# The ninth tile of a pair: two full matmuls into one PSUM bank, and one order for odd and even steps

## Chip, cores, metric

One core of a Trainium2 chip. The metric is the device time of one launch in microseconds (us), the median over runs.

Engine names in the profile: PE is TensorE (PEld its weight loads), DVE VectorE, ACT ScalarE, POOL GpSimd. PSUM is the memory that TensorE writes its products to, in banks; VectorE and ScalarE empty it. A packed matmul uses only part of TensorE's rows or columns (64\*64, 64\*128 or 64\*32 in the profile's rows, against 128\*128 for a full one); going from one of these sizes to another is called a mode switch below.

## The reference, cut to what matters

For 8 batches of 8 heads, 576 positions and head size 64, a memory attention with 32 slots per head, then a layer norm and a feed-forward block over the 512 joined channels, with a residual:

```python
k_m = einsum('bhsm,bhsd->bhmd', a, k)      # a: softmax of phi over positions
v_m = einsum('bhsm,bhsd->bhmd', a, v)
attn = softmax(q @ k_m.T / 8)              # 576 x 32 for each head
x = (attn @ v_m)                           # joined over heads: 8 x 576 x 512
out = x + relu(layernorm(x) * g @ w_ch1) @ w_ch2     # 512 -> 2048 -> 512
```

## The kernel before

It runs in one step per batch. A pair of batches has 2 x 576 = 1152 positions, that is nine tiles of 128. Even steps do tiles 0 to 3, odd steps 4 to 8; hence the "ninth tile" in each odd step. Tile 4 lies across the two batches. A step first makes the hidden layer of its batch (`h_ps`, `mm1`), then for each of its tiles the second product (`ch_ps`, 16 matmuls in two halves, `half(i)`), and in between the attention of the next batch. PSUM is held as two rings: "big" of three buffers of two banks, "one" of two buffers of one bank.

```python
def big(shape, dtype, name):
    return psum.tile(shape, dtype, name=name, tag="big", bufs=3)
def one(shape, dtype, name):
    return psum.tile(shape, dtype, name=name, tag="one", bufs=2)

def x_tiles(pr, ts, stats=True, o_ps=None):        # x of one or two tiles
    n = len(ts)
    if o_ps is None:
        o_ps = big([P, 2, 512], FP32, "o_ps")
    for i, t in enumerate(ts):
        # ... parts: (batch, first and last column, partition offset)
        for g in range(2):
            for (b, a, z, po) in parts:
                s = st8[b]
                for u in range(2):
                    r = 64 * u
                    ov = o_ps[po:po + z - a, u, 256 * i:256 * (i + 1)]
                    nc.tensor.matmul(
                        ov.rearrange("p (j e d) -> p j e d", e=2, d=D)[:, :, g, :],
                        s["Eh"][r:r + 64, g, a:z],
                        s["vb"][r:r + 64, g, 2 * u:2 * (u + 1), :].rearrange("p j d -> p (j d)"),
                        start=True, stop=True, tile_position=(r, po))
    x = moe.tile([P, 2, C], FP32, name="x_sb", bufs=4)
    nc.scalar.activation(out=..., in_=..., func=AF.Copy)      # o_ps to x
    # ...

# ... in the loop over the steps:
half(0)
if more and odd:                     # more: there is a next batch
    o_ps = big([P, 2, 512], FP32, "o_ps")
    kv_ps = big([P, 2, 512], FP32, "kv_ps")
    a_sum(nb, kv_ps)                 # next batch: two small full matmuls
    x_tiles(pr, t[0:2], False, o_ps)
    a_pool(nb, kv_ps)                # 72 packed matmuls; VectorE empties kv_ps
else:
    if more:
        a_kv(nb)                     # a_sum and a_pool
    x_tiles(pr, t[0:2], False)
x_tiles(pr, t[2:4], False)
if odd:
    x_tiles(pr, t[4:5], False)       # the ninth tile
# ... loads
half(1)
x_stats(pr, t[0]); x_stats(pr, t[1]); x_rstd(pr, t[0:2])
if more:
    a_tr(nb)                         # three transposes (kvT_ps)
mm2_out(pr, t[0])                    # VectorE empties the first tile's ch_ps
half(2)
```

`vb` holds zeros outside each head's own block, so contracting over all 128 rows gives the same as contracting each half of 64 rows for its own columns.

The softmax here doesn't subtract the row's maximum and nothing guards it: scores larger than these inputs give would overflow.

## Time and profile before

| | before |
|---|---|
| time | 250.63 us (250.14 to 250.96, 3 runs) |
| TensorE / VectorE / ScalarE busy | 95% / 63% / 52% |
| odd step's stretch, from the batch sums to the second half | 2.21 us |
| even step's | 1.64 us |

The change touches the odd step's stretch, and its like in the last step, which has no next batch. The lines behind the table are in the prediction.

### The profile page before, as it was taken

How to read it: one execution, taken by the hardware profiler on the slowest of the kernel's cores; microseconds unless marked ns; L12 is line 12 of the kernel's file. 1: busy time of each engine (PE TensorE's matmuls, PEld its weight loads, DVE VectorE, ACT ScalarE, POOL GpSimd, SP SyncE). 2: the span in 40 equal slices, each digit the busy share in tenths (PEclk: the TensorE clock that was granted, in tenths of full speed). 3: DMA queues.
4: the chain of work that ended last, by engine and by line, in shares of the span. 5: the costliest groups of instructions: out<-in, count | busy, mean ns of one | idle time of the engine just before them, and what ended most of it. 6: DMA issues, size and time to landing. Idle time of an engine off the chain costs nothing.

```text
span 248.8 us, 5860 instructions
## 1 busy us (share of the span) xinstructions
PE 236.5 (95%) x2460; PEld 132.2 (53%) x2491; DVE 156.0 (63%) x304; ACT 130.0 (52%) x219; POOL 60.7 (24%) x100
## 2 busy tenths in 40 slices
PE   7979899999999999999999999999999999999994
PEld 2544554457544665467544674466544764476442
DVE  3247663685577656687569637685679538783641
ACT  3164572587554465837472656655580755465310
POOL 8643241022325402090206202170205001000000
PEclk9999999999999999999999999999999999999999
DMA  7999999998499799919965997429983301203133
GB/s 150 190 202 206 207 256 213 286 223 148 119 174 236 116 216 245 179 20 194 262 122 117 146 242 168 104 37 221 211 167 68 73 14 43 45 12 75 42 84 84
DMA packets 42451, 36.82 MB, mean 148 GB/s; under 512 B 17461, under 2 KB 37689, under 8 KB 42425
## 3 DMA queue, kind: packets, MB, share of 16 engines
q0 software_dynamic: 17776, 19.53, 46.9%
q1 hardware_dynamic: 24488, 16.79, 28.4%
q8 instruction: 19, 0.31, 0.5%
q10 hardware_dynamic: 160, 0.13, 0.2%
q14 instruction: 8, 0.06, 0.1%
HBM read 41.42 MB, written 9.44 MB: 204 GB/s over the span
## 4 chain that ended last, share of the span: by engine, by line
PE 77%; DMA 17%; issue 2%; ACT 2%; POOL 1%; DVE 0%; POOLq 0%
PE ch_ps L481 45%; PE h_ps L411 22%; DMA q_bf<-in_q_dram 8%; DMA w1r<-in_moe_w_ch_dram 6%; DMA kv_bf<-in_k_dram 3%; PE w1b_ps L390 3%; PE o_ps L442 2%; PE last_ps L493 1%; ACT x_sb L448 1%; PE sc_ps L328 1%; PE den_ps L359 1%; PE kv_ps L210 1%; POOL q_bf L92 1%; PE qT_ps L310 0%; ACT qT L313 0%
## 5 line engine op out<-in xcount | busy, mean ns | idle before, releaser
L481 PE MATMUL ch_ps<-w2b,rT 128*128 128x512 bf16 x531 | 123.0, 379 | 2.3 <-issue 1.6
L481 PEld LDWEIGHTS <-rT 128*128 128x128 bf16 x560 | 52.1, 98 | 63.5 <-issue 6.5
L411 PE MATMUL h_ps<-Eh,w1b 128*128 128x288 bf16 x512 | 66.4, 285 | 1.3 <-ACT rT L417 1.0
L417 ACT ACTIVATE rT<-h_ps 128x576 bf16<-128x576 f32 x88 | 52.2, 648 | 26.8 <-PE h_ps L411 26.8
L411 PEld LDWEIGHTS <-w1b 128*128 128x128 bf16 x512 | 49.5, 97 | 18.1 <-issue 2.4
L394 DVE SCALAR_TENSOR_TENSOR w1b<-m_sb,rsum,w1b_ps 128x512 bf16<-128x512 f32 (+1 forms) x66 | 44.2, 726 | 8.5 <-PE w1b_ps L390 6.1
L419 DVE TENSOR_SCALAR rT<-h_ps 128x576 bf16<-128x576 f32 x40 | 30.3, 758 | 25.2 <-PE h_ps L411 24.6
L505 DVE SCALAR_TENSOR_TENSOR x_sb<-ch_ps,rstd,x_sb 128x512 f32<-128x512 f32 x35 | 26.1, 745 | 9.5 <-PE ch_ps L481 6.4
L461 DVE BATCH_NORM_STATS2 bst<-x_sb 128x6 f32<-128x512 f32 x36 | 24.3, 676 | 6.4 <-ACT x_sb L448 6.4
L448 ACT ACTIVATE x_sb<-o_ps 128x1024 f32<-128x1024 f32 (+1 forms) x20 | 17.8, 939 | 16.1 <-PE o_ps L442 16.0
L287 POOL TENSOR_TENSOR vb<-v,vmask 128x256 bf16<-128x256 bf16 x12 | 7.8, 664 | 60.9 <-DVE rs L237 60.9
L194 POOL TENSOR_TENSOR es<-e_sb 128x512 f32<-128x512 bf16 x6 | 6.9, 1156 | 62.2 <-ACT e_sb L187 62.2
L467 ACT ACTIVATE rstd<-mv,eps_sb 128x2 f32<-128x2 f32 (+1 forms) x20 | 5.9, 297 | 30.8 <-DVE mv L462 30.6
L333 ACT ACTIVATE E_sb<-sc_ps,rs 128x640 bf16<-128x640 f32 x16 | 11.8, 790 | 12.8 <-PE sc_ps L328 12.8
L375 DVE SCALAR_TENSOR_TENSOR Eh<-E_sb,rs,rden 128x576 bf16<-128x576 bf16 x16 | 12.4, 814 | 8.8 <-ACT rden L374 8.8
L179 PE MATMUL w_ps<-fill 128*128 128x512 f32 (+1 forms) x16 | 10.5, 774 | 1.6 <-DVE fill L119 1.6
L227 DVE CAST k<-kv_ps 128x256 bf16<-128x256 f32 x7 | 3.0, 425 | 13.8 <-PE kv_ps L210 13.8
L390 PE MATMUL w1b_ps<-w1r,kvT 64*32 64x512 bf16 (+1 forms) x264 | 10.9, 374 | 0.1
L187 ACT ACTIVATE e_sb<-phi_st 128x1152 bf16<-128x1152 f32 x8 | 9.2, 1151 | 2.7 <-DMA phi_st<-in_phi_dram 2.7
L374 ACT ACTIVATE rden<-rden 128x576 f32<-128x576 f32 x16 | 10.0, 672 | 0.1
L92 POOL DMA_DIRECT2D q_bf<-in_q_dram x10 | 7.6, 757 | 4.6 <-DMA w2b<-in_moe_w_ch_dram 1.8
L210 PE MATMUL kv_ps<-kv_bf,e_sb 64*32 64x128 bf16 (+1 forms) x648 | 7.4, 215 | 0.7 <-DMA kv_bf<-in_v_dram 0.4
(76 smaller groups left out, 150.9 us busy)
## 6 DMA issues: line engine op xcount, KB each, us to landing
out_dram<-x_sb SPq DMA_DIRECT2D x70, 128.0 KB, 2.9
kv_bf<-in_k_dram POOLq DMA_DIRECT2D x7, 576.0 KB, 6.1
kv_bf<-in_v_dram POOLq DMA_DIRECT2D x7, 576.0 KB, 9.5
phi_st<-in_phi_dram SPq DMA_DIRECT2D x6, 576.0 KB, 4.9
q_bf<-in_q_dram POOLq DMA_DIRECT2D x6, 576.0 KB, 13.6
w2b<-in_moe_w_ch_dram POOLq DMA_DIRECT2D x4, 512.0 KB, 17.8
w1r<-in_moe_w_ch_dram POOLq DMA_DIRECT2D x3, 512.0 KB, 14.2
q_bf<-in_q_dram POOLq DMA_DIRECT2D x4, 288.0 KB, 12.6
```

Of the source, the lines that this page charges most:

```text
L179: nc.tensor.matmul(w_ps[:, 0:N], fill[:, 0:P], fill[:, 0:N], start=True, stop=True)
L333: nc.scalar.activation(out=E_[:, g].rearrange("p (a x) -> p a x", a=2), in_=sc[:, :, 0:HP], func=AF.Exp, scale=s["rs"][:, g:g + 1])
L375: nc.vector.scalar_tensor_tensor(out=Eh[:, g, :], in0=s["E"][:, g, 0:S], scalar=s["rs"][:, g:g + 1], in1=rd[:, g].rearrange("p a x -> p (a ...
L390: nc.tensor.matmul(ps[32 * j:32 * (j + 1), g, 0:N], s["kvT"][r:r + 64, 2, 32 * j:32 * (j + 1)], w1r[r:r + 64, j, fs], start=True, stop=Tru ...
L394: nc.vector.scalar_tensor_tensor(out=s["w1b"][:, g, fs], in0=m_sb[:, fs], scalar=s["rsum"][:, g:g + 1], in1=ps[:, g, 0:N], op0=ALU.mult, o ...
L411: nc.tensor.matmul(h_ps[:, half, 0:HS], s["w1b"][:, g, P * j:P * (j + 1)], s["Eh"][:, g, HS * half:HS * (half + 1)], start=(g == 0), stop= ...
L417: nc.scalar.activation(out=dst, in_=h_ps[:, :, 0:HS], func=AF.Relu)
L419: nc.vector.tensor_scalar(out=dst, in0=h_ps[:, :, 0:HS], scalar1=0.0, scalar2=None, op0=ALU.max)
L448: nc.scalar.activation(out=x[:, 0:n].rearrange("p i (u y) -> p i u y", u=2), in_=o_ps.rearrange("p u (i y) -> p i u y", i=2)[:, 0:n], func ...
L461: nc.vector.bn_stats(out=stt, in_=x)
L481: nc.tensor.matmul(ch_ps, rT[:, j, P * t:P * (t + 1)], w2b[:, j, :], start=(j == 0), stop=(j == JC - 1))
L505: nc.vector.scalar_tensor_tensor(out=x, in0=ch_ps, scalar=rstd, in1=x, op0=ALU.mult, op1=ALU.add)
```

## The change

The intent: before, the ninth tile of an odd step takes a third two-bank buffer for 512 columns, which fit one bank. Two matmuls over all 128 rows write to one bank, so the tile can live in the other ring. With a two-bank buffer less, the odd step no longer needs an order of its own. The copy of the ninth tile is put between the copies of the two pairs, so its bank comes back early.

```diff
+        if mid is not None:
+            mid()                       # in x_tiles, between its matmuls and its copy
...
+    def x_one(pr, t):
+        o_ps = one([P, C], FP32, "o1_ps")
...
+        for g in range(2):
+            nc.tensor.matmul(
+                o_ps.rearrange("p (j e d) -> p j e d", e=2, d=D)[:, :, g, :],
+                s["Eh"][:, g, a:a + P], s["vb"][:, g].rearrange("p j d -> p (j d)"),
+                start=True, stop=True)
+        x = moe.tile([P, 2, C], FP32, name="x_sb", bufs=4)
+        nc.scalar.activation(out=x[:, 0], in_=o_ps, func=AF.Copy)
...
         half(0)
-        if more and odd:
-            o_ps = big([P, 2, 512], FP32, "o_ps")
-            kv_ps = big([P, 2, 512], FP32, "kv_ps")
-            a_sum(nb, kv_ps)
-            x_tiles(pr, t[0:2], False, o_ps)
-            a_pool(nb, kv_ps)
-        else:
-            if more:
-                a_kv(nb)
-            x_tiles(pr, t[0:2], False)
-        x_tiles(pr, t[2:4], False)
-        if odd:
-            x_tiles(pr, t[4:5], False)
+        if more:
+            a_kv(nb)
+        x_tiles(pr, t[0:2], False)
+        x_tiles(pr, t[2:4], False, mid=(lambda: x_one(pr, t[4])) if odd else None)
```

More of the change, by code (lines that the diff above doesn't have):

```diff
@@ L422, with x_tiles @@
     xs = {}
-    def x_tiles(pr, ts, stats=True, o_ps=None):
+    def x_tiles(pr, ts, stats=True, o_ps=None, mid=None):
         n = len(ts)
@@ L456, in x_tiles @@
                 x_stats(pr, t)
+    def x_one(pr, t):
+        o_ps = one([P, C], FP32, "o1_ps")
+        b = 2 * pr + P * t // S
+        a = P * t % S
+        s = st8[b]
+        for g in range(2):
[5 more added lines that the diff above has]
+        nc.scalar.activation(out=x[:, 0], in_=o_ps, func=AF.Copy)
+        mv = moe.tile([P, 2, 2], FP32, name="mv", bufs=4)
+        xs[(pr, t)] = (x[:, 0, :], mv, 0, 1)
     def x_stats(pr, t):
```

## The prediction

> **What bounds the kernel now.** I read the page first (engine shares, then the chain that ended last), then the list of TensorE's waits, then the timeline of one odd and one even step, and last the chain of waits inside the odd step.
>
> ```profile
> span 248.8 us, 5860 instructions
> ...
> PE 236.5 (95%) x2460; PEld 132.2 (53%) x2491; DVE 156.0 (63%) x304; ACT 130.0 (52%) x219; POOL 60.7 (24%) x100
> ...
> PE 77%; DMA 17%; issue 2%; ACT 2%; POOL 1%; DVE 0%; POOLq 0%
> ...
> L448 ACT ACTIVATE x_sb<-o_ps 128x1024 f32<-128x1024 f32 (+1 forms) x20 | 17.8, 939 | 16.1 <-PE o_ps L442 16.0
> ```
>
> TensorE is busy for 95% and makes up 77% of the last chain; the DMA share is the loading at the start. VectorE and ScalarE have a third to a half of the span free, so they matter only where TensorE waits for them.
>
> ```profile
> PE ch_ps L481 <- issue: 1.6, 10, 0.2
> PE h_ps L411 <- ACT rT L417: 1.0, 4, 0.2
> ```
>
> These are among the largest entries of the list of TensorE's waits: nowhere does it wait long. The steps confirm it: the same place of steps 1, 3 and 5 stands at 63.81, 118.69 and 173.58 us, that is 54.88 and 54.89 apart. A period that repeats so exactly is set by TensorE's own order, so the change is worth what it does to TensorE's order and small waits there. The place is the stretch between the first and the second half of the first tile's second product. In step 1 (odd), then step 2 (even):
>
> ```profile
> 62.30 1.67 PE L481 MATMUL ch_ps<-w2b,rT 128*128 128x512 bf16 x7
> 63.81 0.19 PE L251 MATMUL kv_ps<-ones,hl 128*128 128x2 bf16 x2
> 63.93 0.52 PE L442 MATMUL o_ps<-vb,Eh 64*64 64x128 bf16 x12
> 64.38 0.80 PE L210 MATMUL kv_ps<-kv_bf,e_sb 64*32 64x128 bf16 x72
> 65.12 0.74 PE L442 MATMUL o_ps<-vb,Eh 64*128 64x128 bf16 x12
> 66.02 1.67 PE L481 MATMUL ch_ps<-w2b,rT 128*128 128x512 bf16 x7 [0.16 <-issue]
> ```
>
> ```profile
> 93.26 0.19 PE L251 MATMUL kv_ps<-ones,hl 128*128 128x2 bf16 x2
> 93.39 0.80 PE L210 MATMUL kv_ps<-kv_bf,e_sb 64*32 64x128 bf16 x72
> 94.12 0.62 PE L442 MATMUL o_ps<-vb,Eh 64*128 64x128 bf16 x16
> 94.90 1.67 PE L481 MATMUL ch_ps<-w2b,rT 128*128 128x512 bf16 x7 [0.16 <-issue]
> ```
>
> The odd stretch takes 66.02 - 63.81 = 2.21 us, the even one 94.90 - 93.26 = 1.64. (Each second half has 8 matmuls and 7 records; the missing one is the first, so the true starts are one matmul, 0.23, earlier in both, and the bracketed "issue" is no real wait. The difference is not touched.) The odd one has 8 matmuls more, but not only that: its row of 12 at 65.12 hides a hole. Cut to a window, its first 8 end early, and the chain of waits goes through ScalarE:
>
> ```profile
> 65.12 0.40 PE L442 MATMUL o_ps<-vb,Eh 64*128 64x128 bf16 x8
> ```
>
> ```profile
> 64.50 1.03 ACT x_sb L448
> 65.53 0.04 issue
> 65.57 0.29 PE o_ps L442 x4
> ```
>
> The eighth starts at 65.12 + 0.40 - 0.216 (its own recorded length) = 65.30; at the pace of the others the ninth tile's first would start at 65.36. It starts at 65.57, 0.04 after the copy of tiles 4 and 5 out of PSUM ends. So a wait of 0.21 us is there: the ninth tile's two-bank buffer is the one that this copy has to empty. The last step has no next batch, hence a buffer more, and there the 24 matmuls run through:
>
> ```profile
> 226.95 1.67 PE L481 MATMUL ch_ps<-w2b,rT 128*128 128x512 bf16 x7
> 228.55 0.86 PE L442 MATMUL o_ps<-vb,Eh 64*64 64x128 bf16 x24
> 229.34 3.84 PE L481 MATMUL ch_ps<-w2b,rT 128*128 128x512 bf16 x17
> ```
>
> **What the Trainium skill says.** (1) "TensorEngine Tiling (Array Packing)", Key Properties: changing the tiling mode, not just the tile, drains TensorE. The trace agrees in effect: the last full matmul before 228.55 starts at 226.95 + 1.67 - 0.379 = 228.24, and the packed one follows 0.31 later instead of the usual 0.216, so a switch costs about 0.09 us. (2) "TensorE: Matmul & The Clock Gate", Part 3: matmuls in different row groups run concurrently. It agrees: 8 packed matmuls take (0.40 - 0.216) / 7 = 26 ns each, about half of 128 columns at the full matmul's pace (512 columns in 0.216, so 54 ns). A full-height matmul gets no such partner. (3) "PSUM — Partial Sum Buffer", The four PSUM rules: one matmul's output fits one bank of 512 fp32 values. The ninth tile has 512 columns, so one bank holds it; the old form needs two because, says the same page, different row tiles must not write one bank at once. No run here shows that limit. (4) The TensorE page, Architectural detail: ScalarE is strictly first in, first out, so where a copy is put in program order is when it runs.
>
> **The change part by part**, for each of steps 1, 3 and 5:
> - Removed: the wait of 0.21. The one-bank buffer comes from the other ring, in which one of two is free by then; the instruction listing of the changed kernel shows no wait on the ninth tile's matmuls.
> - Removed: one mode switch. Before, full, 64x64, 64x128, 64x32, 64x128, full; after, full, 64x32, 64x64, 64x128, full. Four instead of five: -0.09.
> - Changed: four packed matmuls at 26 to 28 ns (0.11) become two full ones of 256 columns. The pace of a full matmul is 0.42 ns a column (0.216 / 512), so 2 x 0.11 = 0.22, their weight loads hidden as those of the others are. +0.11.
> - Sum: -0.19. A check from the even step, whose order the odd one now has: 1.64, plus 0.14 because tile 4 lies across two batches (12 matmuls take 0.52 - 0.216 + 0.05 = 0.36 where the even step's 8 take 8 x 0.028 = 0.22), plus 0.22 for the ninth tile, is 2.00, against 2.21: -0.21. I take -0.2.
>
> In the last step there is no wait and no batch sum between, so only the third part is left: +0.11, and it lies on TensorE's path to the end. Total: 3 x (-0.2) + 0.11 = -0.5 us. 250.63 - 0.5 = 250.1.
>
> ScalarE's work is the same in sum: the 592 ns copy of the ninth tile (one of the other forms of the L448 group) merely moves ahead of the second pair's. VectorE and the transfers keep their counts.
>
> **The rivals.**
> - A new wait in the other ring. The next tile's product (the half that starts at 67.70) now waits for ScalarE's copy of the ninth tile, by the listing: it takes over that bank. Estimate from the rows: the last pair-one matmul ends some 0.73 later than before, so that copy runs about 65.23 to 66.25, the ninth tile's to 66.86, and the product comes at 67.70 - 0.2 = 67.5. Slack 0.6, no wait. Had the copy stood after both pairs it would end near 67.9, a wait of 0.4 a step, which explains its place between. If the ring instead gave the bank of the first tile, whose reader on VectorE runs from 68.50 to 69.24, it would cost some 1.7 us a step and make 256. The listing speaks against it (ScalarE is named, not VectorE).
> - VectorE gets late. Its statistics of tiles 4 and 5 start with the end of the copy, 66.3 instead of 65.85, and stand in its queue ahead of the copies of the transposed keys. Those then run from about 68.0 instead of 67.90, done by 68.5; the scores need them at 69.3. Slack 0.8. If it failed, the gain would be gone: 250.6 to 251.
> - A transfer eats the gain. The transposed queries that step 2 needs at 98.40 land at 98.14 in the trace, only 0.26 ahead. If TensorE comes 0.2 earlier and the landing does not move with it, at most that step's 0.2 is lost: 250.3. The transfer is set off by the same steps, so I expect most of it to move along.
> - More than the sum: the batch's sums come 0.45 earlier and with them GpSimd's work and the loads behind it. No row shows TensorE waiting for these after the start, so nothing follows.
>
> **Range and chances.** The three runs of before spread over 250.14 to 250.96, more than the effect itself. Centre 250.1; 8 in 10 within 249.4 to 250.8. A gain of 2% is 5 us, ten times all that the stretch can give; a loss of 2% needs a new wait of over 1.2 us in each odd step, of which the listing shows no sign. So 0.5% for faster, 98.5% within, 1% for slower.
>
> **What will show it.** In the changed trace the odd stretch should be near 2.0 us (from the sums to the first recorded second-half matmul) in steps 1, 3 and 5, with the last step's 0.79 (228.55 to 229.34) grown to near 0.9; the chain of waits should no longer pass ScalarE there; and the following product should start without a gap. The step's pitch of 54.88 should shrink by 0.2. The prediction is wrong if the product after the transposes waits for ScalarE's copy, if the scores wait for VectorE, or if the two full matmuls take much more than 0.22, for example through their strided output.

## The result

| | before | after |
|---|---|---|
| median, first rounds (6 runs each) | 250.80 us | 250.09 us |
| ratio | | 0.998 (95%: 0.9956 to 1.0005) |
| again, against 10 runs of before (5 runs) | 250.94 us | 250.12 us |
| ratio | | 0.9968 (95%: 0.9956 to 0.998) |

The ratio was worked out from runs of the same rounds; it is not the ratio of the medians. By the 2% measure the two are the same; the repeat shows a gain of 0.3% that its interval separates from zero.

The first profiled run of the changed kernel could mislead. Its page's span and granted-clock lines:

```profile
span 249.0 us, 5843 instructions
...
PEclk9988999999999999999999999999999999999999
```

That span is 0.2 us longer than the 248.8 of before. But two slices near the start have a lower granted clock, and the last matmul ahead of the first odd stretch starts at 64.40 us, against 63.59 before: 0.81 us lost before any changed instruction has run. In the trace of the repeat the same matmul starts at 63.31 and the span is 247.9. The clock need not be the cause: the trace of run 4 below shows no such slice, and there this matmul starts at 64.41. So single spans, and single times, carry about 1 us of start, for a reason that stays open. The steps do not, so all that follows is read between two points of one trace.

The odd stretch of step 1 after, by the timeline of TensorE (start, length, then engine, line, operation, tiles and count; "L467" is the ninth tile, its one-bank buffer printed as `o_ps`):

```profile
64.62 0.19 PE L251 MATMUL kv_ps<-ones,hl 128*128 128x2 bf16 x2
64.74 0.80 PE L210 MATMUL kv_ps<-kv_bf,e_sb 64*32 64x128 bf16 x72
65.47 0.75 PE L442 MATMUL o_ps<-vb,Eh 64*64 64x128 bf16 x20
66.15 0.39 PE L467 MATMUL o_ps<-vb,Eh 128*128 128x256 bf16 x2
66.59 1.67 PE L499 MATMUL ch_ps<-w2b,rT 128*128 128x512 bf16 x7
```

66.59 - 64.62 = 1.97 us, against 2.21 before. The row of 20 packed matmuls has no hole: its last starts at 65.47 + 0.75 - 0.216 = 66.00. The chain of waits no longer passes ScalarE here; TensorE follows TensorE:

```profile
65.54 0.68 PE o_ps L442 x20
66.22 0.32 PE o_ps L467 x2
```

The last step, where there was no wait to remove, got longer from the packed matmuls to the second half, 229.58 - 228.67 = 0.91 against 0.79:

```profile
228.67 0.75 PE L442 MATMUL o_ps<-vb,Eh 64*64 64x128 bf16 x20
229.35 0.39 PE L467 MATMUL o_ps<-vb,Eh 128*128 128x256 bf16 x2
229.58 3.62 PE L499 MATMUL ch_ps<-w2b,rT 128*128 128x512 bf16 x16
```

And ScalarE's copies in step 1 come in the order intended, which is also that of the program, as point (4) of the prediction has it: tiles 4 and 5, the ninth, tiles 6 and 7.

```profile
66.04 1.02 ACT L450 ACTIVATE x_sb<-o_ps 128x1024 f32<-128x1024 f32 x1 [2.76 <-PE o_ps L442]
66.96 0.59 ACT L472 ACTIVATE x_sb<-o_ps 128x512 f32<-128x512 f32 x1
67.43 1.03 ACT L450 ACTIVATE x_sb<-o_ps 128x1024 f32<-128x1024 f32 x1
```

The ninth tile's copy ends at 66.96 + 0.59 = 67.55; the product that takes over its bank starts at 68.27 in the same trace. That is the 0.7 us of slack on which the change stands.

### The profile page after: what moved, and what is told of

It is laid out like the page before. It is cut to its first block, busy times and chain, and to the rows that moved or that the text cites. A ratio compares the mean times of both kernels' runs of the same rounds, so it can differ in the third digit from the quotient of the medians.

```text
span 249.0 us, 5843 instructions
## 1 busy us (share of the span) xinstructions
PE 237.1 (95%) x2452; PEld 133.0 (53%) x2483; DVE 156.5 (63%) x304; ACT 129.8 (52%) x219; POOL 60.8 (24%) x100
## 4 chain that ended last, share of the span: by engine, by line
PE 89%; DMA 4%; ACT 2%; issue 2%; POOL 1%; DVE 1%; POOLq 0%
PE ch_ps L499 48%; PE h_ps L411 25%; DMA kv_bf<-in_v_dram 4%; PE w1b_ps L390 3%; PE kv_ps L210 2%; PE o_ps L442 2%; PE last_ps L511 1%; PE sc_ps L328 1%; PE m_ps L165 1%; PE den_ps L359 1%; ACT rT L417 1%; PE w_ps L179 1%; POOL q_bf L92 1%; ACT E_sb L333 1%; DVE w1b L394 1%
## 5 line engine op out<-in xcount | busy, mean ns | idle before, releaser
L450 ACT ACTIVATE x_sb<-o_ps 128x1024 f32<-128x1024 f32 x16 | 16.0, 1027 | 18.2 <-PE o_ps L442 18.2
```

What stands on the lines that cost most here:

```text
L450: nc.scalar.activation(out=x[:, 0:n].rearrange("p i (u y) -> p i u y", u=2), in_=o_ps.rearrange("p u (i y) -> p i u y", i=2)[:, 0:n], func ...
```

## The experiments

Each row below is one trace, and the kernels of runs 1 to 5 and 8 were timed once only. To compare traces, I take four numbers from the starts of TensorE's instructions, which the trace gives to the nanosecond. A: from the last matmul of the first half to the first transpose, in steps 1, 3 and 5 (they agree within 0.003 us), free of the missing record. B: the pitch from step 1's stretch to step 2's. C: from the last matmul of the first half to the first recorded one of the second half in the last step. D: from the last matmul of the first half in step 1 to the first matmul of the last product (`last_ps`), that is all that the steps can gain. The even steps, which no run alters, are a check: A taken there lies between 3.361 and 3.364 in every trace.

| kernel | A | B | C | D |
|---|---|---|---|---|
| before | 3.936 | 29.456 | 1.101 | 177.85 |
| the change | 3.705 | 29.227 | 1.218 | 177.26 |
| 1 new tile, old order | 3.811 | 29.333 | 1.217 | 177.57 |
| 2 old tile, new order | 3.904 | 29.424 | 1.100 | 177.75 |
| 3 copy after both pairs | 3.704 | 29.466 | 1.217 | 178.39 |
| 4 ninth tile five times over | 4.578 | 30.100 | 2.092 | 180.77 |
| 5 copy behind the rstd | 3.703 | 30.924 | 1.218 | 184.22 |
| 6 last step packed | 3.703 | 29.226 | 1.101 | 177.15 |
| 6 once more | 3.705 | 29.226 | 1.100 | 177.24 |
| 7 the change again | 3.704 | 29.220 | 1.218 | 177.25 |
| 8 ninth tile between the pairs | 3.916 | 29.433 | 1.419 | 178.10 |

My theory was a sum of three small terms on TensorE: a wait gone, a mode switch less, two full matmuls in place of four packed ones. The rivals: it is all the PSUM wait; it is all the order; the stretch is not on the path that sets the end.

**1. The new ninth tile alone**, in the odd steps' old order:

```diff
-        if more:
-            a_kv(nb)
-        x_tiles(pr, t[0:2], False)
+        # the order of before: a_sum, x_tiles(t[0:2]), a_pool in odd steps
         x_tiles(pr, t[2:4], False, mid=(lambda: x_one(pr, t[4])) if odd else None)
```

> The new ninth tile alone: two full matmuls into one bank, but the odd steps keep the order of before (sums, tiles 4 and 5, the rest of the batch sums, tiles 6 and 7). The stretch is counted from the last recorded matmul of the first half to the first recorded one of the second half: 2.426 us before, 2.194 after the change, in steps 1, 3 and 5. Theory (three terms of TensorE: wait gone -0.22, one mode switch less -0.09, full for packed +0.09): the wait goes, the switch stays, so 2.29. Rival 'all is the PSUM wait, the order is idle': 2.19, as after. Rival 'all is the order': 2.43 or more. Last step 1.218 as after.

The timeline of its step 1 has no hole between the packed eight and the ninth tile:

```profile
65.59 0.40 PE L442 MATMUL o_ps<-vb,Eh 64*128 64x128 bf16 x8
65.92 0.39 PE L467 MATMUL o_ps<-vb,Eh 128*128 128x256 bf16 x2
66.14 1.89 PE L499 MATMUL ch_ps<-w2b,rT 128*128 128x512 bf16 x8
```

A falls by 0.125 us, where 0.136 was expected (as all 8 matmuls of the second half are recorded here, the stretch to the second one, 2.30, is what compares with the expected 2.29; to the first it is 2.08). The wait is gone, but 0.106 us of the change's gain is missing: the size of one switch, which run 8 measures on its own. Neither rival holds: the order is not idle, nor is it all.

**2. The new order alone**, with the packed ninth tile in two banks:

```diff
-        x_tiles(pr, t[2:4], False, mid=(lambda: x_one(pr, t[4])) if odd else None)
+        x_tiles(pr, t[2:4], False)
+        if odd:
+            x_tiles(pr, t[4:5], False)
```

> The new order alone: batch sums first, but the ninth tile stays four packed matmuls into a two-bank buffer. Theory: one switch less (-0.09), but the two-bank buffer is now the one of the batch sums, which VectorE empties last; it reads until about 1.90 us after the start of the stretch, the ninth tile would be ready at 1.66, so a wait of about 0.28 stays: stretch 2.38 in steps 1, 3 and 5. Rival 'all is the order': 2.19. Rival 'the buffer of tiles 4 and 5 is taken': wait on ScalarE's copy, about 3.1. Last step 1.101 as before.

A falls by 0.032 only (0.046 expected). The wait has not gone, it has changed its owner. The chain of waits in step 1 now runs through VectorE's emptying of the batch sums' buffer:

```profile
65.19 0.42 DVE k L227
65.62 0.20 DVE v L232
65.82 0.09 DVE rs L237
65.90 0.05 issue
65.95 0.29 PE o_ps L442 x4
```

By the starts the new wait is 0.30 us (65.95 where 65.65 was due at the usual pace), against the old one of 0.22; the difference eats most of the switch saved. So each pays fully only with the other: the buffer alone is worth 0.28 us (D: 177.85 - 177.57), the order alone 0.10, together 0.59.

**3. The place of the copy**: ScalarE copies the ninth tile last.

```diff
-        x_tiles(pr, t[2:4], False, mid=(lambda: x_one(pr, t[4])) if odd else None)
+        x_tiles(pr, t[2:4], False)
+        if odd:
+            x_one(pr, t[4])
```

> The changed kernel, but ScalarE copies the ninth tile after the second pair instead of between the pairs. Theory: the stretch stays at 2.19, but the product after the transposes takes over the ninth tile's bank, the copy ends about 0.6 (one two-bank copy of 1.02 less the slack of some 0.6) too late, so TensorE waits 0.4 to 0.5 us before it in each odd step, and the step's pitch grows by that: the total is 1.6 to 2.0 us over the changed kernel in the steps. Rival 'the place of the copy is idle': no gap, total as after.

The wait is there, exactly at the end of that copy, but smaller than expected: the product after the transposes comes 0.24 us later in steps 1, 3 and 5 and 0.41 in the last, and D grows by 1.13 against the change where 1.6 to 2.0 was expected. The chain of waits in step 1:

```profile
66.58 1.02 ACT x_sb L450
67.60 0.50 ACT x_sb L472
68.10 0.04 issue
68.14 1.46 PE ch_ps L499 x6
```

My error was to lay the copies end to end, in the prediction too ("a wait of 0.4 a step"). Recorded at 1.02 us each, they start 0.90 to 0.92 apart, so two of them end 0.2 earlier than I had it. The Trainium skill says as much: "Perfetto Trace Analysis", Optimizing Scalar/DVE Operations, notes that a profiled latency contains a write acknowledgement that overlaps with the next instruction. Here that overlap is 0.10 to 0.12 us.

**4. A known cost put in**: the two full matmuls five times over.

```diff
+        for _ in range(5):
             for g in range(2):
                 nc.tensor.matmul(o_ps..., start=True, stop=True)
```

> The changed kernel with the two full matmuls of the ninth tile issued five times over (each time from the start, so the result stays right). Theory: 8 more matmuls of 256 columns at 0.109 us are 0.87 us in each of the four odd steps, all on TensorE's path: stretch 3.07 in steps 1, 3 and 5, last step 2.09, total 3.5 us over the changed kernel. Rival 'the strided write into the bank is slow, hidden in the drain': more than 0.109 each. Rival 'the stretch is not on the path that sets the end': the stretch grows, the pitch of the steps does not.

```profile
66.16 1.27 PE L468 MATMUL o_ps<-vb,Eh 128*128 128x256 bf16 x10
67.26 1.03 PE L500 MATMUL ch_ps<-w2b,rT 128*128 128x512 bf16 x4
```

A and C grow by 0.87 each, so eight more matmuls cost 0.109 us apiece. That is also the distance of matmuls of 256 columns with an unbroken output in the trace of before (those into `m_ps`, before the steps), so this strided write to the bank costs nothing. B grows by the same 0.87 and D by 3.5: what the stretch gains or loses arrives whole at the end. The profiled run took 254.27 us, 4.60 more than the 249.67 of the profiled run of the repeat below; 3.5 of that is D, and 1.1 lies before step 1 (64.41 against 63.31 in the two traces).

**5. The bank held longer**: the ninth tile's copy is put behind the first tile's rstd on ScalarE.

```diff
         mm2_out(pr, t[0])
+        if odd:
+            held[0]()          # x_one hands its copy back (cut here); it is issued only now
         half(2)
```

> The changed kernel, but the ninth tile's copy is put behind the first tile's rstd on ScalarE. Theory: the bank comes free about 1.1 us after the rstd's start, some 1.7 us after TensorE wants it, so a gap of 1.5 to 1.8 us before the product after the transposes in steps 1, 3 and 5 and a similar one in the last: total 6 to 7 us over the changed kernel. It sizes the rival of the prediction in which the new wait in the one-bank ring is late. Rival 'another bank is given': no gap.

TensorE waits where the prediction's first rival put it, before the product after the transposes:

```profile
69.30 1.02 PE L501 MATMUL ch_ps<-w2b,rT 128*128 128x512 bf16 x4 [1.54 <-ACT x_sb L473]
```

The idle time of 1.54 us is shorter than the loss because the transposes' modelled ends reach into it; by starts the product comes 1.70 later in steps 1, 3 and 5 and 1.87 in the last, so D grows by 6.96, and the time is 257.06. The prediction had made it "256" if the bank came back only behind the first tile's reader; with the ninth tile's copy behind the rstd it is of that size. So the change hangs on which reader frees the bank (ScalarE by the compiled instruction listing that the prediction cites; the traces of runs 3 and 5 show the same) and on where that copy stands.

**6. The last step packed**, as there the two-bank buffer is free:

```diff
-        x_tiles(pr, t[2:4], False, mid=(lambda: x_one(pr, t[4])) if odd else None)
+        x_tiles(pr, t[2:4], False, mid=(lambda: x_one(pr, t[4])) if odd and more else None)
+        if last:
+            x_tiles(pr, t[4:5], False)
```

> The changed kernel, but in the last step, where no batch sums need a buffer, the ninth tile stays packed in two banks as before. Theory: the stretch of steps 1, 3 and 5 is 2.194 as after, the last step's 1.10 as before; the gain in the steps is 3 x 0.232 = 0.70 us against 0.58 for the changed kernel, so a ratio to before of about 0.9972. Rival 'the last step needs the bank too': over 1.2 in the last step. A difference of 0.12 to the changed kernel will not show in the times, only in the trace.

```profile
227.90 0.86 PE L442 MATMUL o_ps<-vb,Eh 64*64 64x128 bf16 x24
228.69 4.49 PE L499 MATMUL ch_ps<-w2b,rT 128*128 128x512 bf16 x20
```

The steps do as expected: C is 1.101 again and D falls by 0.70 against before. The times did not: ratio 0.9992 (0.9963 to 1.002), median 250.33, with two of six runs at 251.25 and 252.03 us. Only one of these runs has a trace, so what held the two up is not shown by it; their granted clocks, 0.999 and 0.986, don't agree on a reason. The interval still holds the expected 0.9972. I timed it again:

> The version with the packed ninth tile in the last step once more: its first timing had two runs of over 251 us among six. Theory: those were slow starts, not the steps: by the trace again 3 x 0.231 = 0.69 us less than before between step 1 and the last product, ratio to before 0.996 to 0.998. Rival 'this version has something slow of its own': again 0.999 or more.

This time the ratio is 0.9965 (0.9952 to 0.9978), median 249.94 us, no run over 250.21. So it is no slower than the change, and nothing of its own shows in the steps. Whether it is faster, the times cannot say: 0.12 us is under their noise. The trace says 0.12 us less in the last step. D of this second trace is 177.24, as one other thing happened in it: the scores of step 2 started 0.09 us late, 0.14 after the landing of the transposed queries (97.99 us) that they read. In the traces of runs 4 and 6 the scores of step 2 also start 0.135 us after this landing, held by less than 0.01. The trace bears it out: the scores' first weight load waits for the semaphore of this transfer and is let go at 98.02, 0.03 after the landing. So it is the prediction's third rival, met with 0.09 us once.

**7. The change once more**, in the rounds of 6:

> The changed kernel once more, beside the one before it in the same rounds. Theory: stretches as in its first trace to 0.01 us (2.194, last step 1.218), ratio to before 0.9977; the first slices may differ with the granted clock. Rival 'the 0.998 was drift': ratio 1.000.

A, B and C repeat to 0.007 us, the ratio is 0.9968. Drift falls.

**8. The price of a mode switch**: the same instructions, with the ninth tile's two full matmuls between the packed pairs on TensorE, too.

```diff
         x_tiles(pr, t[0:2], False)
-        x_tiles(pr, t[2:4], False, mid=(lambda: x_one(pr, t[4])) if odd else None)
+        if odd:
+            x_one(pr, t[4])
+        x_tiles(pr, t[2:4], False)
```

> The changed kernel, but TensorE too computes the ninth tile between the two pairs (its copy stands there already). Theory: the same instructions with two more changes of tiling mode (packed to full and back), nothing else, so the stretch from the last matmul of the first half to the transposes grows from 3.705 by two switches of 0.09 to 3.89 in steps 1, 3 and 5, and the last step's from 1.22 to 1.40. Rival 'a switch costs nothing, the full matmuls' slower pace explains the gap': 3.705 as after. No new wait, the copy comes earlier.

```profile
64.75 0.52 PE L442 MATMUL o_ps<-vb,Eh 64*64 64x128 bf16 x12
65.20 0.39 PE L467 MATMUL o_ps<-vb,Eh 128*128 128x256 bf16 x2
65.53 0.40 PE L442 MATMUL o_ps<-vb,Eh 64*128 64x128 bf16 x8
65.86 1.90 PE L499 MATMUL ch_ps<-w2b,rT 128*128 128x512 bf16 x8
```

A grows by 0.21, C by 0.20: 0.10 to 0.11 us a switch, a little over the 0.09 expected. Two switches in the wrong place undo nearly all that the change gains in an odd step (B is 29.433 against 29.456 before), and with the last step D, 178.10, is above the 177.85 of before.

## Why the prediction was right

Predicted 250.1 us in a range of 249.4 to 250.8, "within 2%"; measured 250.09, and 250.12 in the repeat. That the medians hit is partly luck: single runs spread over more than the effect, and the base that the prediction started from (250.63, three runs) was 250.80 and 250.94 in the rounds compared, where the medians differ by 0.71 and 0.82. The sum of the steps is the better test: -0.59 us (D) where -0.5 was predicted. Point by point:

- *TensorE's order sets the time.* Right. The odd-to-even pitch is the same within 0.004 us in steps 1, 3 and 5 of the trace of before and within 0.002 after the change, and a cost of known size (run 4) came out whole.
- *A hidden wait of 0.21 on the copy of tiles 4 and 5.* Right. It is gone in run 1, and run 2 shows that without the smaller buffer it moves to VectorE instead. The Trainium skill, "Perfetto Trace Analysis", Optimization Strategy, says that the same gap repeating on the engine that should be saturated can mean too little PSUM for the next tile; this was one, of 0.2 us in each odd step with a next batch, and a merged timeline row hid it.
- *A switch less, 0.09.* Right in kind, a little small: 0.10 to 0.11 by runs 1 and 8.
- *Full for packed, +0.11.* Measured +0.117 in the last step, where nothing else changed.
- *Sum -0.2 for an odd step.* Measured -0.231. The terms as measured give -0.22 - 0.105 + 0.117 = -0.21; about 0.02 is left. Of that, 0.014 is seen: after the wait the four packed matmuls started over 0.073 us, in the last step, without a wait, over 0.059. The rest is not settled.
- *No new wait in the other ring.* Right, with 0.7 us of slack where 0.6 was estimated. Runs 3 and 5 show that the wait is real and would come out in full; for a copy after both pairs the prediction's 0.4 a step was too much, as 0.24 was measured (run 3).
- *VectorE late but in time.* Right. Counted from the last matmul of the first half, its statistics start 0.43 us later (2.69 for 2.26), but the copies of the transposed keys only 0.01 (4.31 for 4.30). After the change it finishes the copies of the transposed keys at 69.17 (68.89 + 0.28), and the scores start at 70.09, a slack of 0.9 where 0.8 was estimated.
- *The transfer moves along.* Mostly: the transposed queries landed 0.24 to 0.34 us ahead of the scores in both traces of the change, of which some 0.135 us are needed (run 6). In the second trace of run 6 they were 0.09 us too late.
- *Nothing from the earlier batch sums.* Right. GpSimd's next product (`vb`) starts 0.45 us earlier (1.89 for 2.35, counted as above), but of the 0.59 by which D falls, A and C alone give 3 x 0.231 - 0.117 = 0.58.

## What to carry to other kernels

When one engine is full, look inside merged rows of its timeline: a group whose length does not fit its count times its pace hides a wait, and the chain of waits names its owner. A smaller buffer only helps if its new ring gives it back in time; ask which reader frees that bank, and put that reader early in its queue. And where the expected gain is 0.2% and the start alone varies by 1 us, measure the steps in the trace and not the run.

## What the Trainium skill lacked or had wrong

- "TensorEngine Tiling (Array Packing)", Key Properties: it says that a change of tiling mode drains TensorE, without a figure. Here one switch cost 0.09 us by starts of neighbouring matmuls (0.309 for 0.216) and 0.10 to 0.11 by taking one out or putting two in (runs 1 and 8).
- "PSUM — Partial Sum Buffer", Specifications: it says that any non-contiguous access pattern slows matmuls significantly. Here an output in four runs of 64 columns did not: such matmuls of 256 columns took 0.109 us each (run 4), as did those with an unbroken output. Shorter runs were not tried.
- "Perfetto Trace Analysis": it does not warn that the first matmul record of a group can be absent. In the first traces of both kernels only 531 of the 560 matmuls of the second product are recorded, and the second half has 7 records of 8, which shifts a stretch by 0.22 us; in the later traces all are there.
